# Reordering SyncE's final DMA waits by the age of each lane's last transfer, in a windowed-attention and SwiGLU kernel

## Chip, cores, metric

One core of one Trainium2 chip. The metric is device microseconds (us) of one execution. The span in a profile, from the first to the last instruction, is about 1.8 us shorter than that time.

## The reference, cut to what matters

```python
# q, k, v: (8, 8, 576, 64) float32; window 64, causal
scores = scale * (q @ k^T), masked to 0 <= i - j < 64
x = softmax(scores) @ v                      # -> (4608, 512)
out = (silu(x @ w_gate) * (x @ w_val)) @ w_out   # d_ff 1536, out (4608, 512) float32
```

What matters is the end: the output leaves in 128-row blocks, and the program may only end when the last of them is in HBM.

## The kernel before: the parts that matter

The kernel records its operations in a list, finds the dependencies, and gives every DMA a *lane*. A lane is one semaphore. The DMAs of a queue take its lanes in turn: 16 lanes for the GpSimd queue, 16 for SyncE's, up to 8 for ScalarE's (it issues only two DMAs, so two lanes). `lanes` remembers the last DMA of each lane, and, being a dictionary, keeps the order in which the lanes were *first* used. (The comments in the cuts below are added; the kernel itself has none there.)

```python
            if o.dma:
                nl = self.LANES[e]
                o.lane = (e, ndma[e] % nl)
                o.occ = ndma[e] // nl
                ndma[e] += 1
                prev = lanes.get(o.lane)
                if prev is not None:
                    need(prev)
                lanes[o.lane] = o          # a lane keeps its first place in the dict
    # ... cut ...
        def run(eng, e):
            # ... each engine's own instructions and waits ...
            if e == "sp":
                for lane, o in lanes.items():      # at SyncE's end: wait for every lane
                    k, v = target(o)
                    eng.wait_ge(sem[k], v)
```

The last 128 rows are stored in three pieces, the first two from SyncE's queue and the last from ScalarE's:

```python
    def O_last(self, c, u):
        # ... cut ...
        for c0, c1, eng, q in ((0, 256, "act", "sp"), (256, 384, "act", "sp"), (384, 512, "dve", "act")):
            # 12 matmuls into a bank, eviction by eng to ost, then:
            g.op(q, lambda e, d=d, c0=c0, c1=c1: e.dma_start(self.out[r0:r0 + 128, c0:c1], d), ...)
```

The softmax here doesn't subtract the row's maximum and nothing guards it: scores larger than these inputs give would overflow.

## Time and profile before

337.33 us, the median of 3 executions (337.13 to 337.44). The profiled execution is none of these three: it took 336.34 us.

From the page of the kernel before: the span, the busy time of each engine, part of the table in 40 slices (each digit is tenths of a slice; PEclk is the clock granted to TensorE), and the chain that ended last.

```profile
span 334.5 us, 8436 instructions
PE 320.5 (96%) x3532; PEld 171.0 (51%) x3568; DVE 212.8 (64%) x451; ACT 138.9 (42%) x256; POOL 110.8 (33%) x141
...
PE   7979998999999999999999999999999999999996
...
PEclk9989999999999999999999999999999999999999
...
PE 82%; DMA 7%; POOL 4%; DVE 3%; issue 2%; ACT 1%; SPq 1%; POOLq 0%
```

TensorE is busy nearly everywhere. In the last slice it is at 6 tenths: that is the tail, in which only the last eviction, the last store and the closing waits are left. The timeline of the kernel before for that tail (start in us, duration in us, what):

```profile
331.27 0.33 SPq L649 DMA_DIRECT2D out_dram<-ost  x1
331.33 0.27 PE L641 MATMUL ps<-Wo,hT 128*128 128x128 bf16 x2
331.64 0.29 DVE L296 COPY ost<-ps 128x128 f32<-128x128 f32 x1 [11.84 <-PE ps L641]
331.96 0.36 ACTq L649 DMA_DIRECT2D out_dram<-ost  x1
```

The last instruction shown starts at 331.96, yet the span ends at 334.54. The rest is on SyncE's own queue, which the busy table does not count. By source line, in the kernel before: the wait instructions at SyncE's end (line 140), and of line 142, the closing barrier, SyncE's part. Columns: line, engine, operation and count; duration in ns (least/median/most); first and last start.

```profile
L140 SPq EVENT_SEMAPHORE  x17: 17/28/28, 331.7 to 334.1; - x17
...
L142 SPq COMPARE_BRANCH  x1: 41/41/41, 334.1 to 334.1; - x1
L142 SPq DRAIN  x1: 7/7/7, 334.3 to 334.3; - x1
L142 SPq EVENT_SEMAPHORE  x1: 17/17/17, 334.5 to 334.5; - x1
```

And what SyncE waited for from 330 us on, in the kernel before (us in total, times, longest):

```profile
SPq L140 <- DMA out_dram<-ost: 1.5, 2, 0.8
SPq L649 <- ACT ost L294: 1.0, 2, 0.7
SPq L142 <- PEq L142: 0.2, 1, 0.2
```

The 17 wait instructions last 2.4 us, but only two of them really wait, together 1.5 us. The others pass at once. Where do they stand? The built program of the kernel before shows it (not a profile; each cell is one instruction after SyncE's last store; the semaphores that the trace records with these instructions give the same order):

```
d_pool15 | d_sp1,d_pool14 | d_sp2,d_pool13 | d_sp3,d_pool12 | d_sp4,d_pool11 | d_sp5,d_pool10 |
d_sp6,d_pool9 | d_sp7,d_pool8 | d_sp8,d_pool7 | d_sp9,d_pool6 | d_sp10,d_pool5 | d_sp11,d_pool4 |
d_sp12,d_pool3 | d_sp13,d_pool2 | d_sp14,d_pool1 | d_sp15,d_pool0 | d_act1,d_act0 | branch: d_sp0
```

The 34 waits of the source have become 17 instructions with up to two waits each, and one wait on the branch. They also stand in another order than written: the middle of the list comes first, and the rest follows outward from both sides. SyncE's last two stores are in lanes 6 and 7, ScalarE's, the last of all, in `d_act1`. Eight instructions, nine steps, lie between `d_sp7` and `d_act1`.

A DMA has *landed* when the last of the 16 increments of its semaphore has come. The last store landed at 333.703 us. The wait instructions of the kernel before that start between then and the branch:

```profile
L140 SPq EVENT_SEMAPHORE  x7: 27/28/28, 333.7 to 334.1; - x7
```

The Trainium skill, "Perfetto Trace Analysis", section "Identifying Dependency Chains", says that an instruction waiting on several engines may have EventSemaphore instructions with the further conditions inserted before it. This trace agrees: 17 of them stand before the branch, which carries the last wait itself.

### The profile page before, as it was taken

How to read it: one execution, taken by the hardware profiler on the slowest of the kernel's cores; microseconds unless marked ns; L12 is line 12 of the kernel's file. 1: busy time of each engine (PE TensorE's matmuls, PEld its weight loads, DVE VectorE, ACT ScalarE, POOL GpSimd, SP SyncE). 2: the span in 40 equal slices, each digit the busy share in tenths (PEclk: the TensorE clock that was granted, in tenths of full speed). 3: DMA queues.
4: the chain of work that ended last, by engine and by line, in shares of the span. 5: the costliest groups of instructions: out<-in, count | busy, mean ns of one | idle time of the engine just before them, and what ended most of it. 6: DMA issues, size and time to landing. Idle time of an engine off the chain costs nothing.

```text
span 334.5 us, 8436 instructions
## 1 busy us (share of the span) xinstructions
PE 320.5 (96%) x3532; PEld 171.0 (51%) x3568; DVE 212.8 (64%) x451; ACT 138.9 (42%) x256; POOL 110.8 (33%) x141
## 2 busy tenths in 40 slices
PE   7979998999999999999999999999999999999996
PEld 7748567554444545454545454545454544444444
DVE  5548789578547757676767676666666666555510
ACT  2645874355425525343434343434352522232222
POOL 7999993373527132515143423200000000000000
PEclk9989999999999999999999999999999999999999
DMA  9999999999999999899979797941514111100012
GB/s 170 151 191 173 165 197 134 142 190 142 174 185 156 165 188 118 140 109 144 110 120 134 119 136 112 143 125 34 128 33 126 30 66 33 65 31 31 31 65 95
DMA packets 169510, 40.15 MB, mean 120 GB/s; under 512 B 155904, under 2 KB 164992, under 8 KB 169472
## 3 DMA queue, kind: packets, MB, share of 16 engines
q0 software_dynamic: 117312, 18.36, 77.0%
q1 hardware_dynamic: 50976, 20.66, 29.2%
q10 hardware_dynamic: 1184, 0.59, 0.6%
q8 instruction: 28, 0.46, 0.5%
q14 instruction: 10, 0.08, 0.1%
HBM read 37.75 MB, written 9.44 MB: 141 GB/s over the span
## 4 chain that ended last, share of the span: by engine, by line
PE 82%; DMA 7%; POOL 4%; DVE 3%; issue 2%; ACT 1%; SPq 1%; POOLq 0%
PE ps L584 50%; PE ps L611 25%; PE ps L408 3%; DMA qT<-qn 2%; DMA xT<-xb 2%; PE ps L515 2%; DMA Wv<-in_moe_w_val_dram 2%; POOL va L339 1%; PE ps L458 1%; DVE uu L592 1%; PE ps L641 1%; POOL Wg L345 1%; POOL qn L277 1%; POOL kn L277 1%; POOL Wv L345 0%
## 5 line engine op out<-in xcount | busy, mean ns | idle before, releaser
L592 DVE SCALAR_TENSOR_TENSOR uu<-sig,ps 128x512 bf16<-128x512 bf16 (+2 forms) x122 | 76.2, 625 | 69.7 <-ACT sig L590 69.5
L584 PE MATMUL ps<-xT,Wv 128*128 128x512 bf16 (+2 forms) x486 | 113.7, 356 | 1.7 <-DMA Wv<-in_moe_w_val_dram 1.6
L584 PE MATMUL ps<-xT,Wg 128*128 128x512 bf16 (+2 forms) x468 | 109.7, 355 | 4.0 <-issue 1.0
L590 ACT ACTIVATE sig<-ps 128x512 bf16<-128x512 f32 (+2 forms) x122 | 67.0, 549 | 85.5 <-PE ps L584 85.4
L611 PE MATMUL ps<-Wo,hT 128*128 128x512 bf16 x406 | 95.0, 379 | 2.1 <-issue 2.1
L594 DVE SCALAR_TENSOR_TENSOR hT<-uu,ps 128x512 bf16<-128x512 bf16 (+2 forms) x122 | 76.3, 626 | 5.6 <-PE ps L584 1.4
L584 PEld LDWEIGHTS ps<-xT,Wv 128*128 128x128 bf16 x488 | 47.3, 98 | 48.5 <-DMA Wv<-in_moe_w_val_dram 1.8
L584 PEld LDWEIGHTS ps<-xT,Wg 128*128 128x128 bf16 x488 | 45.9, 98 | 47.4 <-DMA xT<-xb 0.9
L611 PEld LDWEIGHTS ps<-Wo,hT 128*128 128x128 bf16 x420 | 40.0, 98 | 46.6
L277 POOL DMA_DIRECT2D qn<-in_q_dram x38 | 35.1, 939 | 76.9 <-DMA qT<-qn 76.7
L418 ACT ACTIVATE pt<-ps 128x512 bf16<-128x512 f32 x72 | 37.7, 600 | 26.3 <-PE ps L408 26.3
L623 ACT ACTIVATE ost<-ps 128x512 f32<-128x512 f32 x35 | 20.9, 597 | 66.7 <-PE ps L611 66.5
L339 POOL DMA_DIRECT2D va<-in_v_dram x40 | 36.8, 928 | 18.6 <-PE ps L515 17.9
L277 POOL DMA_DIRECT2D kn<-in_k_dram x38 | 35.0, 926 | 5.1 <-DMA Wo<-in_moe_w_out_dram 5.1
L424 DVE TENSOR_TENSOR pt<-pt,mask 128x512 bf16<-128x512 bf16 x64 | 23.4, 419 | 3.3 <-ACT pt L418 3.2
L537 DVE TENSOR_TENSOR xb<-ps,rp 128x448 bf16<-128x448 f32 (+1 forms) x36 | 18.5, 513 | 1.2
L534 DVE RECIPROCAL rp<-ps 128x7 f32<-128x7 f32 (+1 forms) x36 | 6.7, 187 | 15.4 <-PE ps L515 15.4
L408 PE MATMUL ps<-qT,kT 64*64 64x64 bf16 (+1 forms) x864 | 16.0, 203 | 0.5 <-DMA qT<-qn 0.5
L408 PEld LDWEIGHTS ps<-qT,kT 64*64 64x64 bf16 x864 | 12.4, 108 | 7.3 <-DVE hT L594 4.2
L515 PE MATMUL ps<-va,pt 64*64 64x65 bf16 x728 | 11.5, 193 | 0.1
L476 DVE TENSOR_TENSOR xb<-ps,rc 128x256 bf16<-128x256 f32 x24 | 10.2, 425 | 0.8
L515 PEld LDWEIGHTS ps<-va,pt 64*64 64x64 bf16 x728 | 9.4, 108 | 0.6 <-DVE hT L594 0.4
(46 smaller groups left out, 92.3 us busy)
## 6 DMA issues: line engine op xcount, KB each, us to landing
out_dram<-ost SPq DMA_DIRECT2D x35, 256.0 KB, 3.0
va<-in_v_dram POOLq DMA_DIRECT2D x32, 128.0 KB, 10.0
qn<-in_q_dram POOLq DMA_DIRECT2D x30, 128.0 KB, 10.1
kn<-in_k_dram POOLq DMA_DIRECT2D x30, 128.0 KB, 6.4
Wo<-in_moe_w_out_dram POOLq DMA_DIRECT2D x2, 768.0 KB, 15.9
Wg<-in_moe_w_gate_dram POOLq DMA_DIRECT2D x5, 256.0 KB, 8.0
Wv<-in_moe_w_val_dram POOLq DMA_DIRECT2D x5, 256.0 KB, 9.2
fk<-in_k_dram SPq DMA_DIRECT2D x1, 512.0 KB, 5.1
```

The lines of the kernel that those rows point to most:

```text
L277: self.g.op("pool", lambda e, d=d, a=a: e.dma_start(d, a), writes=ks, dma=True)
L339: g.op("pool", lambda e, d=d, a=a: e.dma_start(d, a), writes=ks, dma=True)
L408: r = e.matmul(sv[h][o:o + 64, c, q0:q1], self.kT[ps, c, kk:kk + 64], qT[ps, c, q0:q1], start=not biased, stop=not biased or c == 3 and kk ...
L418: g.op("act", lambda e, po=po, si=si: e.activation(po, si, ACTF.Exp, scale=SCALE), reads=[bk], writes=[pk])
L424: "dve", lambda e: e.tensor_tensor(po, po, m, ALU.mult), reads=[pk, "mask"], writes=[pk]))
L515: r = e.matmul(bb[b][0][ws, 65 * sl:65 * sl + 65], self.pt[(n + j) % self.NP][ks, h, ws], vv[ks, h, 0:65], start=m == q[0], stop=m == q[-1])
L584: r = e.matmul(bank[:, 0:n], W[:, kk, f * 128:f * 128 + 128], xT[:, kk, t0:t1], start=(kk == 0), stop=(kk == NK - 1))
L590: g.op("act", lambda e: e.activation(sig[:, 0:n], G[:, 0:n], ACTF.Tanh, scale=0.5), reads=[gk], writes=[("sig", i)])
L592: g.op("dve", lambda e: e.scalar_tensor_tensor(uu[:, 0:n], sig[:, 0:n], 1.0, G[:, 0:n], ALU.add, ALU.mult), reads=[("sig", i), gk], writes ...
L594: g.op("dve", lambda e: e.scalar_tensor_tensor(hT[:, f, t0:t1], uu[:, 0:n], 0.5, V[:, 0:n], ALU.mult, ALU.mult), reads=[("uu", i), vk], wr ...
L611: r = e.matmul(OB[:, :], hT[:, f, 128 * u:128 * u + 128], self.Wo[:, f, :], start=(f == 0), stop=(f == NF - 1))
L623: g.op("act", lambda e: e.activation(ost[:, :], OB[:, :], ACTF.Copy), reads=[ok], writes=[("ost", io)])
```

## The change

The intent is that the last store's lane is waited for last, so that no satisfied wait stands behind it, but for the one on the branch, which runs in any case.

```diff
             if e == "sp":
-                for lane, o in lanes.items():
+                for lane, o in sorted(lanes.items(), key=lambda x: x[1].i):
                     k, v = target(o)
                     eng.wait_ge(sem[k], v)
```

That is the whole diff. No other instruction changes or moves.

## The prediction

> **What bounds the kernel now.** TensorE. The page's busy table has PE busy 320.5 of 334.5 us (96%), and 82% of the chain of waits is PE. The two built programs hold the same instructions in the same order on all engines, waits aside. Only the last 2.9 us can change. There, from the timeline and SyncE's records: last matmul ends at 331.6, VectorE's last eviction 331.64 to 331.93, ScalarE issues the last store at 331.96 (64 KB; its last engine's write lands 333.70). SyncE issues its last two stores at 330.71 and 331.27; they land at 332.82 and 333.52. The program ends after SyncE has been through 34 waits for DMA lanes, then a barrier, at 334.54.
>
> **What the change moves.** The source has 34 single waits; both built programs hold them as 17 wait instructions and a branch that carries the last one. The written order is not kept: it starts from the middle of the list and goes outward in pairs. So in the kernel before the order is SyncE lanes 1 to 15 (each with a lane of the GpSimd queue), then the ScalarE lane of the last store, then SyncE lane 0 on the branch. The last SyncE stores lie in lanes 6 and 7. The trace's SyncE records show: five pairs go by 60 to 73 ns apart, then the lane-6 pair waits until 332.835 and the lane-7 pair until 333.533 (17 ns after each landing); nine pairs later, 61 ns apart, ScalarE's lane is asked for at 334.078. It had landed at 333.703, so 0.375 us are spent on satisfied waits. Then 0.46 us of branch, drain and barrier.
>
> After the change the order outward from the middle is SyncE lanes 8 to 15, 0 to 5, then 6, 7, then ScalarE's last store; the branch carries ScalarE's old lane. The first 14 need 14 x 0.061 = 0.85 us from 331.66, so they are over by about 332.5, before anything lands. Then lane 6 at 332.835, lane 7 at 333.533, ScalarE's lane at about 333.72 (landing plus 17 ns), branch about 333.785 instead of 334.143. The rest moves up by **0.36 us** (span about 334.18).
>
> The Trainium skill, page "DMA: Bandwidth & Descriptors", section "Anatomy of one DMA", puts a fixed cost of about 2.0 us on a DMA, mostly the write receipt. This trace agrees (2.1, 2.2 and 1.7 us from issue to landing of the last three stores). The order of waits cannot shorten that.
>
> **Critical path.** All 0.36 us are on it, but that is 0.1% of the time.
>
> **Predicted time: 337.0 us, range 336.4 to 337.6** (the three runs before spread over 0.3 us). Chances: faster by over 2%: 0.005; within 2%: 0.99; slower by over 2%: 0.005.
>
> **What would show it right.** SyncE's wait records after its last store: 14 waits close together ending near 332.5, then three that each begin within 20 ns of a landing, and the branch 65 ns after the last; span ending 0.48 us after the last landing instead of 0.84. Everything before 331.6 unchanged. **Wrong:** satisfied waits still standing between the last landing and the branch, or the last store landing later than 1.75 us after its issue.
>
> **What would make it wrong.** A landing that varies from run to run by more than 0.3 us, which hides the gain; a ScalarE store that lands before SyncE's lane 7 (then the saving grows to at most about 0.5 us); a clock state.

## The result, and the profile after

335.91 us median (335.63 to 336.90, 6 executions), against 337.26 us (336.98 to 338.73, 6 executions) for the kernel before. The ratio is 0.9958 with a 95% interval of 0.9936 to 0.998. Ratios here are the mean time of one kernel's fast executions over that of the other's in the same rounds, so not quite the ratio of the medians.

So the time fell by 1.35 us by the medians. The prediction had said 0.36 us, and a range of 336.4 to 337.6 us, which does not hold 335.91.

The profile after, the lines that answer to those above; first the page:

```profile
span 334.3 us, 8472 instructions
PE 323.9 (97%) x3568; PEld 170.8 (51%) x3568; DVE 212.8 (64%) x451; ACT 139.0 (42%) x256; POOL 110.7 (33%) x141
...
PE   8979989998899999999999999999999999999996
...
PEclk9999999999999999999999999999999999999999
...
PE 84%; DMA 7%; POOL 4%; DVE 2%; ACT 1%; issue 1%; SPq 1%; POOLq 0%
```

(The counts of PE differ because matmul records are missing from the trace before; the weight loads, 3,568 in both, show that the work is the same.) The profiled executions differ by only 0.2 us in span, far less than the medians. The timeline of the tail of the changed kernel:

```profile
331.78 0.29 DVE L296 COPY ost<-ps 128x128 f32<-128x128 f32 x1 [11.83 <-PE ps L641]
332.10 0.36 ACTq L649 DMA_DIRECT2D out_dram<-ost  x1
```

The changed kernel came to its tail 0.14 us *later* than the kernel before, and ended 0.24 us *earlier*. SyncE's closing instructions in the changed kernel, by source line, and what it waited for from 330 us on:

```profile
L140 SPq EVENT_SEMAPHORE  x17: 17/28/28, 331.8 to 333.8; - x17
...
L142 SPq COMPARE_BRANCH  x1: 41/41/41, 333.9 to 333.9; - x1
L142 SPq DRAIN  x1: 7/7/7, 334.1 to 334.1; - x1
L142 SPq EVENT_SEMAPHORE  x1: 17/17/17, 334.2 to 334.2; - x1
```

```profile
...
SPq L140 <- DMA out_dram<-ost: 1.0, 2, 0.7
SPq L649 <- ACT ost L294: 1.0, 2, 0.8
SPq L142 <- PEq L142: 0.2, 1, 0.2
```

And the wait instructions of the changed kernel that start after the last store's landing (333.822 us), one in place of seven:

```profile
L140 SPq EVENT_SEMAPHORE  x1: 28/28/28, 333.8 to 333.8; - x1
```

The trace's records of SyncE give each start and landing (us from the span's start):

| | before | after |
|---|---|---|
| last matmul ends | 331.602 | 331.744 |
| ScalarE issues the last store | 331.964 | 332.104 |
| wait instruction with lane `d_sp6` passes | 332.835 | 332.878 |
| wait instruction with lane `d_sp7` passes | 333.533 | 333.651 |
| last engine's write of the last store lands | 333.703 | 333.822 |
| wait instruction with lane `d_act1` passes | 334.078 | 333.837 |
| branch | 334.143 | 333.902 |
| end of the span | 334.539 | 334.300 |
| **landing to end** | **0.836** | **0.478** |
| **tail: last matmul's end to end** | **2.937** | **2.556** |

Before, SyncE works off nine steps of 59 to 62 ns after `d_sp7`, and comes to `d_act1` 0.375 us after the store has landed. After, it is already standing there and passes 15 ns after the landing. The landing to the end is 0.358 us shorter, which is the predicted size to the second digit. The predicted mechanism is in the trace. The 1.35 us are not.

### The profile page after: what moved, and what is told of

It reads as the page before. It is cut to its first block, busy times and chain, and to the rows that moved or that the text cites. A ratio compares the mean times of both kernels' runs of the same rounds, so it can differ in the third digit from the quotient of the medians.

```text
span 334.3 us, 8472 instructions
## 1 busy us (share of the span) xinstructions
PE 323.9 (97%) x3568; PEld 170.8 (51%) x3568; DVE 212.8 (64%) x451; ACT 139.0 (42%) x256; POOL 110.7 (33%) x141
## 4 chain that ended last, share of the span: by engine, by line
PE 84%; DMA 7%; POOL 4%; DVE 2%; ACT 1%; issue 1%; SPq 1%; POOLq 0%
PE ps L584 50%; PE ps L611 26%; PE ps L408 3%; DMA qT<-qn 3%; PE ps L515 2%; DMA xT<-xb 2%; DMA Wv<-in_moe_w_val_dram 2%; POOL va L339 1%; PE ps L458 1%; PE ps L641 1%; POOL Wg L345 1%; PE ps L364 1%; POOL qn L277 1%; POOL kn L277 1%; DVE uu L592 0%
## 5 line engine op out<-in xcount | busy, mean ns | idle before, releaser
L584 PE MATMUL ps<-xT,Wg 128*128 128x512 bf16 (+2 forms) x488 | 113.5, 355 | 2.0 <-DMA Wg<-in_moe_w_gate_dram 0.8
L611 PE MATMUL ps<-Wo,hT 128*128 128x512 bf16 x420 | 98.0, 379 | 0.0
```

The lines of the kernel that those rows point to most:

```text
L584: r = e.matmul(bank[:, 0:n], W[:, kk, f * 128:f * 128 + 128], xT[:, kk, t0:t1], start=(kk == 0), stop=(kk == NK - 1))
L611: r = e.matmul(OB[:, :], hT[:, f, 128 * u:128 * u + 128], self.Wo[:, f, :], start=(f == 0), stop=(f == NF - 1))
```

## The experiments

Two theories of the missing 1 us were put against each other.

- **Theory A**: the order moves the tail alone. The rest of the measured difference is scatter of the part of the execution ahead of the tail, which the change does not touch.
- **Theory B** (later **E**, a version limited to some sessions): the new order makes the whole execution shorter by another 1 us, by some way not seen.

Two further rivals concern the tail itself: **C**, what costs is the number of waits, wherever they stand; and **D**, the waits run in the order in which they are written.

Three sessions were run, on three different chips. In each the kernel before was executed 11 times as well. In every experiment "ahead of the tail" means the span of an execution less the tail of that kernel's profile. That takes the tail for constant, which is good to some 0.03 us: three profiles of the order before gave 2.937, 2.930 and 2.940, three of the changed order 2.556, 2.564 and 2.590.

### e1_same: the kernel before, against itself

No edit.

> The kernel before, unchanged, timed against itself. Theory A (the change shortens only the tail after the last store's landing, by 0.36 us; the rest of the measured 1.35 us is scatter of the load phase from execution to execution): ratio 1.000 with an interval of about 0.002 either way, single executions scattered over 1 us or more, tail from the last matmul's end to the end of the span 2.94 us. Theory B (the new order of the waits makes the whole execution about 1.3 us shorter each time): ratio 1.000 as well, but with single executions that never reach below 336.5 us.

Measured: 336.19 us median (335.30 to 337.90, 7 executions), against 336.62 us (335.41 to 337.93, 11 executions) of the same program. Ratio 0.9984, interval 0.9957 to 1.0011. Tail 2.930 us. The executions of one unchanged program lie 2.6 us apart, and the shortest are well below 336.5 us, so theory B's limit falls. The three executions that the prediction's range was built on had spread over 0.3 us.

### e2_again: the changed kernel once more

No edit to the changed kernel.

> The changed kernel, unchanged, timed a second time on this chip. Theory A: ratio 0.9989, anywhere from 0.997 to 1.0005, tail 2.56 us. Theory B: ratio 0.996 once more, interval clear of 0.9985.

Measured: 335.95 us median (335.26 to 337.53, 6 executions), ratio 0.999, interval 0.996 to 1.002. Tail 2.564 us. The ratio is theory A's 0.9989 to three digits, though the interval does not shut out 0.996. It is also not clear of 0.9985, as theory B wanted.

### e3_late: the last store's lane early

```diff
-                for lane, o in lanes.items():
+                age = sorted(lanes.items(), key=lambda x: x[1].i)
+                for lane, o in age[:16] + age[-1:] + age[16:-1]:
```

> The waits reordered so that the ScalarE lane of the last store stands in the second wait instruction; 15 instructions with lanes that have then all landed follow it. Theory A: 15 x 0.061 us = 0.92 us more tail than the changed kernel, 0.56 us more than before: tail about 3.5 us, ratio 1.0017. Theory B (any order other than the old one is shorter by its effect on the execution): ratio below 1.000.

Measured: 337.35 us median (336.10 to 337.89, 6 executions), ratio 1.0018, interval 0.9991 to 1.0045. Tail 3.469 us, 0.91 more than after the change and 0.53 more than before, where 0.92 and 0.56 were expected. SyncE's waits in this kernel from 329 us on:

```profile
...
SPq L141 <- DMA out_dram<-ost: 2.0, 1, 2.0
...
```

One long wait instead of two, and then 15 satisfied instructions behind it. The order alone, with the same number of waits, moves the end of the program in either direction. This is read from the tails; the interval of the time does not exclude 1.

### e4_few: seven waits in place of 34

```diff
-                for lane, o in lanes.items():
+                age = sorted(lanes.items(), key=lambda x: x[1].i)
+                for lane, o in age[-7:]:
```

> Only the seven youngest lanes are waited for (27 of 34 waits taken away; those lanes' transfers are all consumed long before), the last store's lane in the last wait instruction. Theory A: the 14 instructions that the changed kernel has before the first landing cost nothing, so the tail is as in the changed kernel, 2.56 us, ratio 0.9989. Rival C (what costs is the number of waits, wherever they stand): 14 x 0.061 = 0.85 us less than the changed kernel, tail 1.7 us, ratio 0.9964.

Measured: 336.08 us median (334.95 to 336.40, 6 executions), ratio 0.9982, interval 0.9956 to 1.0007. Tail 2.525 us; landing to end 0.482 us, against 0.478 in the changed kernel. By source line, the wait instructions at the end of this kernel:

```profile
L141 SPq EVENT_SEMAPHORE  x3: 28/28/28, 331.7 to 332.7; - x3
```

Fourteen fewer instructions than in the changed kernel, and the same landing to end. Rival C wanted a tail of 1.7 us and falls.

### e5_pad: 108 satisfied wait instructions behind the landing

```diff
-                for lane, o in lanes.items():
+                age = sorted(lanes.items(), key=lambda x: x[1].i)
+                old = age[:-7]
+                for lane, o in 4 * old + age[-7:] + 4 * old:
```

> The changed order, with the 27 old lanes waited for eight times over, placed so that 108 wait instructions for long-landed lanes stand behind the one with the last store's lane. Theory A (each satisfied wait instruction behind the last landing costs 0.061 us, wherever the rest of the program stands): 108 x 0.061 = 6.6 us more than the changed kernel, tail about 9.1 us, time about 342.4 us, ratio to before 1.0185. A theory in which SyncE's waits at the end don't count expects no change.

Measured: 342.93 us median (342.51 to 344.24, 4 executions) against 336.40 us, ratio 1.0202, interval 1.0169 to 1.0236. Tail 9.54 us, against 9.1 expected. By source line, the wait instructions of this kernel from the landing on:

```profile
L142 SPq EVENT_SEMAPHORE  x109: 27/28/28, 334.0 to 340.9; - x109
```

An instruction lasts 28 ns, but they start 59 to 62 ns apart: the step is the cost, not the duration. Six of the steps were longer (67 to 384 ns), together about 0.4 us over the usual step, and that is the excess over the expected tail; what held them up is not known. (This trace alone has an eleventh packet on the instruction queue q14, 8 KB, at 339.13 us, some 0.4 us after the last of these steps; that the two belong together is not shown.) The whole time follows: a cost of 0.061 us that no mean over ten executions would show is seen clearly when it is taken a hundred times.

### e6_young_first: the list sorted the other way round

```diff
-                for lane, o in lanes.items():
+                for lane, o in sorted(lanes.items(), key=lambda x: -x[1].i):
```

> The list sorted the other way round, youngest lane first. Theory A with the built order (outward from the middle of the list, two to an instruction) puts the last store's lane on the branch, after all else: tail 2.56 less one step of 0.065 = 2.50 us, ratio 0.9987. Rival D (the written order is what runs): the last store is waited for first and 16 to 17 wait instructions follow it, tail about 3.5 us, ratio 1.0018.

Measured: 335.94 us median (335.41 to 337.27, 4 executions), ratio 0.9994, interval 0.9965 to 1.0023. Landing to end 0.417 us, 0.06 less than with the change, as expected. The tail was 2.614 us and not 2.50, because in this one profile the last store took 1.835 us from issue to landing in place of 1.718 in the profile after; the waits have no part in that. Rival D wanted a tail of 3.5 us and falls: written youngest first, the list ends as well as written oldest first, because it is built outward from its middle and both ends come last.

### e7_six: six waits, the last store on the branch

```diff
-                for lane, o in lanes.items():
+                young = sorted(lanes.items(), key=lambda x: -x[1].i)[:6]
+                for lane, o in [young[j] for j in (0, 4, 5, 3, 2, 1)]:
```

> Only the six lanes that nothing else in the program waits for, written so that the last store's lane lands on the branch. Theory A: tail 2.50 us, about 0.43 us less than before and 0.06 less than the changed kernel, ratio 0.9987 with the scatter of about 0.003 around it. Rival C (number of waits): far less, tail 1.6 us.

Measured: 335.78 us median (334.80 to 336.92, 6 executions), ratio 0.9985, interval 0.9958 to 1.0012. Tail 2.518 us, landing to end 0.410 us. This is the shortest landing to end of all the kernels, 0.07 us below the changed kernel's. The execution time does not resolve that gain. Rival C wanted a tail of 1.6 us.

### e8_hidden: 14 more wait instructions, ahead of the landing

```diff
-                for lane, o in lanes.items():
+                age = sorted(lanes.items(), key=lambda x: x[1].i)
+                for lane, o in age[:17] + age[:14] + age[:14] + age[17:]:
```

> The changed order with 14 more wait instructions for long-landed lanes put in front, where SyncE stands idle until the last store lands. Theory A: 28 instructions x 0.061 = 1.7 us from the last issue, over before the last landing (2.06 us after it in the changed kernel), so nothing is added: tail 2.56 us, ratio 0.9989. Rival C: 14 x 0.061 = 0.85 us more, tail 3.4 us, ratio 1.0014.

Measured: 336.34 us median (335.75 to 337.13, 4 executions), ratio 1.0001, interval 0.9974 to 1.0029. Tail 2.579 us, landing to end 0.477 us. By source line, the wait instructions at the end of this kernel:

```profile
L141 SPq EVENT_SEMAPHORE  x31: 17/28/28, 331.4 to 333.5; - x31
```

31 wait instructions instead of 17, in a stretch of the same length: the 14 more went into time in which SyncE was waiting anyway. Together with e5_pad this is the answer to rival C from the other side. The ratio missed theory A's 0.9989 by 0.0012, inside its interval. These four executions were the longest ahead of the tail, 332.02 us on average against 331.75 for all.

### e9_changed_third and e10_before_third: a third session

No edits. One thing was still open: the six executions of the kernel before in the first comparison were all at 336.98 us or above, and most of its later ones were not.

> The changed kernel in a third session, because the six executions of the kernel before in the first comparison were all longer (336.98 us and up) than most of the 29 executions of it in the two sessions since. Theory A (the order moves the tail alone, and the first comparison drew long executions of the kernel before): ratio 0.9989, between 0.996 and 1.001; the part of the span ahead of the tail averages 331.7 us as in all kernels so far. Rival E (in some sessions the old order costs the rest of the execution another 1 us): ratio 0.996 with the part ahead of the tail 1 us shorter than in the kernel before of the same session.

> The kernel before against itself in the same session. Theory A: ratio 1.000 within 0.003, tail 2.93 us, the part ahead of the tail 331.7 us on average, within 0.5. Rival E: about 1 us above the changed kernel's in that part.

Measured: changed kernel 336.14 us median (335.39 to 337.16, 6 executions), ratio 0.9992, interval 0.9965 to 1.0019, tail 2.590 us. Kernel before against itself 336.19 us (335.36 to 338.24, 6 executions), ratio 1.0001, interval 0.9971 to 1.0032, tail 2.940 us. Theory E expected 0.996 in a session that has what the first had; this third one, like the two before it, has not.

### All executions together

| kernel | executions | mean time, us | landing to end, us | tail, us | ahead of the tail, mean, us |
|---|---|---|---|---|---|
| before, session 1 | 11 | 336.60 | 0.84 | 2.94 | 331.86 |
| before, session 2 | 11 | 336.35 | 0.84 | 2.94 | 331.62 |
| before, session 3 | 11 | 336.51 | 0.84 | 2.94 | 331.80 |
| e1_same | 7 | 336.31 | 0.843 | 2.930 | 331.58 |
| e10_before_third | 6 | 336.51 | 0.837 | 2.940 | 331.79 |
| after, first comparison | 6 | 336.05 | 0.478 | 2.556 | 331.68 |
| e2_again | 6 | 336.18 | 0.478 | 2.564 | 331.82 |
| e9_changed_third | 6 | 336.23 | 0.485 | 2.590 | 331.84 |
| e3_late | 6 | 337.12 | 1.383 | 3.469 | 331.85 |
| e4_few | 6 | 335.90 | 0.482 | 2.525 | 331.59 |
| e5_pad | 4 | 343.15 | 7.424 | 9.538 | 331.84 |
| e6_young_first | 4 | 336.14 | 0.417 | 2.614 | 331.74 |
| e7_six | 6 | 335.84 | 0.410 | 2.518 | 331.52 |
| e8_hidden | 4 | 336.39 | 0.477 | 2.579 | 332.02 |

(The three rows "before" have no profile of their own in those sessions; the tail of the order before is taken for them. The six executions of the kernel before in the first comparison, mean 337.47 us, are not in the table: their spans are not on record. Less 1.8 and 2.94 us, about 332.7 us ahead of the tail is an estimate for them.)

The last column is the result. Eight different orders and numbers of waits give the same time ahead of the tail, 331.52 to 332.02 us, while single executions in it run from 330.4 to 333.6 us, with a standard deviation of 0.74 us. Theory B needed the kernel before to be 1 us above the others in this column: its 46 executions here average 331.74 us, the 48 of all other orders 331.75 us.

Where does that scatter arise? Early. In the twelve profiles, the 1,601st of the 3,568 weight loads starts between 122.07 and 124.53 us, 2.5 us apart. From there to the end of the last matmul all twelve take 208.52 to 208.78 us, 0.26 us apart. So the first 123 us, in which the DMA engines are busiest (169 GB/s up to 124 us in the kernel before, 91 GB/s from there to 320 us), hold nearly all of it. The waits of TensorE between 15 and 125 us differ from profile to profile of the same program. The kernel before, its first profile, in part (us in total, times, longest):

```profile
PE ps L584 <- DMA Wv<-in_moe_w_val_dram: 1.6, 1, 1.6
...
PE ps L584 <- DMA Wg<-in_moe_w_gate_dram: 0.5, 1, 0.5
```

The kernel before, the profile in e1_same, in part:

```profile
PE ps L584 <- DMA Wg<-in_moe_w_gate_dram: 2.2, 2, 1.5
PE ps L408 <- ACT xT L559: 1.5, 1, 1.5
...
PE ps L408 <- DMA qT<-qn: 1.0, 1, 1.0
PE ps L584 <- DMA Wv<-in_moe_w_val_dram: 0.7, 1, 0.7
```

The same program waits for other weights, and for other lengths, in two executions. Which of these comes first, and why, was not tried.

## Why the prediction was right or wrong

- **The built order of the waits, the 0.375 us of satisfied waits behind the landing, the 61 ns step, 14 waits over before the first landing**: right. The last of the 14 stood at 332.597 us, "near 332.5" in the prediction; the next three passed 15 to 16 ns after their landings; the branch followed 65 ns later; the span ended 0.478 us after the landing, where 0.48 was said.
- **The gain of 0.36 us**: right. The landing to the end went from 0.836 to 0.478 us, and each of the six profiles of the two orders shows it to 0.01 us. The time alone does not show it: the 46 later executions of the kernel before average 336.46 us and the 12 later ones of the changed kernel 336.21 us, 0.26 us less, with a standard error of 0.25 us from the scatter of both. What a longer tail does to the time is shown by e5_pad, whose mean is 6.80 us above the kernel before's of its session, where its tail is 6.60 us longer.
- **The range, 336.4 to 337.6 us, "the three runs before spread over 0.3 us"**: wrong, and this is the step that failed. It took the spread of three executions for the spread of the kernel. The 46 later executions of the same program run from 335.10 to 338.24 us. The point prediction was also taken from those three, whose median, 337.33 us, lies 0.9 us above the later mean. The profiled execution of the kernel before, 336.34 us, lies below all three and just below the range. The prediction's own span, 334.18 us, plus the 1.8 us, gives 335.98 us, beside 335.91 us measured; with this scatter, so close an agreement is partly luck.
- **"Everything before 331.6 unchanged"**: not so in the sense of times. The instructions are the same, but the last matmul ended at 330.64 to 333.17 us in the twelve profiles. The prediction named scatter of a landing as a danger; the last store took 1.68 to 1.84 us in all twelve, 0.15 us apart, and the 2.5 us of scatter lie ahead of the tail.
- **"Another 1 us" in the first comparison**: by the means, 337.47 less 336.05 is 1.41 us. Of that 0.36 to 0.38 us is the tail. The other 1.0 us is on the side of the kernel before: its six executions average 337.47 us, the 46 later ones of the identical program 336.46 us, while the changed kernel's 336.05 us agrees with its later 336.21 us (12 executions). So the interval of that first ratio, 0.9936 to 0.998, did not hold the effect that the tails show, 0.9989 (337.33 less 0.36, over 337.33).
- **What stays open**: why those six were all long, so the cause of this 1.0 us. Only 14 of the 46 later executions reach 336.98 us, so six of six is more than a mere draw would give if executions of a session were independent. Something of that occasion may have acted on them. Three further sessions on three chips did not show it again, so it could not be examined.
- **"A ScalarE store that lands before SyncE's lane 7"**: did not occur. In all twelve profiles it landed last.

## What to carry to other kernels

At the end of a program, look at which satisfied waits stand *behind* the one that ends last; here each was a step of about 61 ns of SyncE on the critical path, and those in front of it cost nothing as long as they were over before it ended. (Whether waits in the middle of a program behave alike was not tried.) Read the order from the built program or the trace, not from the source: here the list was built outward from its middle, and its reverse did as well. And before setting a range from a few executions, ask whether they can show the scatter: here a 0.36 us gain that is plain in every profile would need some forty executions of each kernel to stand two standard errors clear in the time (0.8 us of standard deviation for one execution), and the first comparison, with a narrow interval, showed almost four times as much.

## What the Trainium skill lacked or had wrong

- No page gives the cost of a satisfied wait instruction on SyncE. The runs show a step of mostly 59 to 62 ns (58 to 73 ns among the first five of a list, and longer in six steps of e5_pad), of which the instruction itself lasts 17 to 28 ns, and a blocked one starting 15 to 17 ns after the landing in the profiles before and after. The nearest is "Advanced Engine Details and Errata", section "Network/Comms", which puts reading a semaphore from the sequencer at 50 to 100 ns: the step agrees with that in size, but the page does not say that it is meant for a wait.
- "Perfetto Trace Analysis", section "Identifying Dependency Chains", mentions inserted EventSemaphore instructions, but not that waits written one after the other are put together in twos and reordered. Here 34 waits became 17 instructions and a branch, outward from the middle of the list.
- "DMA: Bandwidth & Descriptors", section "Anatomy of one DMA — SWDGE (gpsimd) path", gives about 2.0 us of fixed cost, for the GpSimd path, which none of the last stores takes; that section has no total for the queues of SyncE and ScalarE. The 64 KB store from ScalarE's queue at the end took 1.68 to 1.84 us from issue to landing in twelve profiles; one of the same size from SyncE's queue took 2.2 us in the profiles before and after. They are measurements of another path and no test of the page's figure.
- "TensorE: Matmul & The Clock Gate", section "What's actually happening", describes a half clock and windows of 3,413 ns. The traces agree (a stretch of 3.41 us at half clock, starting between 21.5 and 23.8 us, in six of the nine profiles that have a clock record), but no page says what the executions show: those listed with a mean clock under 0.997 were the *shorter* ones (37 executions without those of e5_pad, 331.33 us ahead of the tail on average, against 332.03 us for the other 53). e5_pad is left out because its profile has no such stretch: its mean clock is low from the half clock in its long tail. Three profiles (e1_same, e6_young_first, e7_six) have no clock record and are listed with clock 1.0, so the group of 53 may hold others like them. Why is open; a lower granted clock is not by itself the sign of a longer execution here.
